# Four reorderings in a fused routing-attention and tanh-shrink kernel: a row of codes ahead of streamed factors, six stores on another queue, one rounding later, routing ahead of one-hot masks

## The chip, the cores and the metric

The kernel runs on one core of a Trainium2 chip. The metric is the device time of one execution in microseconds (us). The core has five engines that run their own instruction streams and wait for each other by semaphores: PE (TensorE, matrix products), DVE (VectorE), ACT (ScalarE), POOL (GpSimd) and SP (SyncE, which here only issues DMAs). Transfers are issued by SP, ACT or POOL, each in its own order, and are carried out by 16 DMA engines.

## The reference

Two blocks follow each other. The first is attention in which a query sees only the keys of its own cluster; the second is a feed-forward layer with the activation h - tanh(h).

```python
# q, k, v: (4, 8, 768, 64); centroids: (8, 16, 64)
q_assign = argmax(q_n @ c_n.T); k_assign = argmax(k_n @ c_n.T)   # per head, 16 clusters
scores = where(q_assign == k_assign, q @ k.T / sqrt(64), -1e9)
attn = softmax(scores)
x = (attn @ v)  -> (3072, 512)          # heads side by side
h = x @ w_in                            # (512, 2048)
out = (h - tanh(h)) @ w_out             # (2048, 512)
```

The weights arrive as 64-bit floats and are rounded to 32 bits on the chip.

## The kernel before, in words

**Steps.** Two heads make a pair; there are 16 pairs, four for each of the four batches. A pair is worked in two halves of 384 queries, and each half in three steps of two blocks of 128 keys. A list `steps` puts them in order: first the halves 0 of pairs 0 to 3 (steps 0 to 11), then their halves 1 (steps 12 to 23), then pair after pair (from step 24). The loop `for at, (n, half, s) in enumerate(steps)` writes out every engine's instructions by hand (`manual_schedule`): the order in the program is the order on each engine and each queue.

In step `at`, PE computes the scores of step `at + 1` (`begin`, line 501), ACT takes their exponentials (line 523), DVE sets those of other clusters to zero (`select`, line 533, which compares a `row` of query codes with a key's code), and PE multiplies the weights of step `at` with the values (`value`, line 558). Between these stand parts of the feed-forward layer (`fill`).

**Masks and codes.** `before(n)` lists the stages of a pair before its first step: turn, `similar` (PE, line 377), `turn_back`, `route` and `route_on` (DVE, lines 387 to 415: the code of each query and key), `publish` (DVE line 432, and a store of the codes by SP, line 436). Pairs 1 to 3 in half 0 have no `select`; PE adds a mask product (line 512) from a one-hot tile `hot`. For that `spread_both` (SP, line 465) reads the codes back into `hot`, and `one_hot` (DVE, lines 476 and 480) turns them into a mask. In step 4 both the one-hot of pair 2 (stage 5) and the routing of pair 3 (stage 2) are due. For the other halves `spread` (SP, lines 448 and 456) fetches a row of codes two to five steps ahead.

**Rounding.** The weights come as 32 pieces. `fetch` asks for one on POOL's queue (line 218), `rest_of` (ACT, lines 150 and 151) and `round_piece` (DVE, lines 159 and 162) round it, and `round_piece` then fetches the piece three further on. `paces` says how many pieces each step rounds.

**Factors.** From batch 0's second half on, the feed-forward products use seven products in place of eight, with sums of quarters of the weights as factors. In steps 20 to 22 `up_maker(0)` and `up_maker(1)` (the index is `q`) make four sums each on DVE (line 833), and `keep` stores these and three plain quarters (numbers 1, 2 and 4, read straight from `w_in`) into `up_factors` in DRAM, each in two DMAs of 256 KB (line 797). The 22 items are dealt out over the three steps, eight, seven and seven. `fetch_factors` (line 856) streams them back into the freed tiles of `w_in`, 896 KB at a time, the first two in step 21 and the next in step 24, where PE begins to use them (`up_product`, line 925; DVE adds in line 920). At the start of step 24 DVE also computes differences of the right side (`right_factors`, line 891) into `w_in[3]`.

Of the kernel before, what the change touches and what calls it, by code (L numbers as in the profile page):

```python
# [58 lines left out]
def kernel(  # L59
# [10 lines left out]
    nc = tc.nc  # L70
# [109 lines left out]
    def fast():  # L180
# [291 lines left out]
        def one_hot(n: int):  # L472


            t = hots[n]
            nc.vector.tensor_scalar(
                out=t[:, 1], in0=t[:, 1], scalar1=mine_code, scalar2=-FAR,
                op0=ALU.not_equal, op1=ALU.mult,
            )
            nc.vector.tensor_scalar(  # L480
                out=t[:, 0, 0], in0=t[:, 0, 0], scalar1=mine_code, scalar2=None, op0=ALU.is_equal
            )
# [42 lines left out]
        def select(n: int, half: int, j: int):  # L525

            if not masked(n, half):
                if j % 2 == 0 and not summed(n, half):
                    weights[n, half, j // 2] = weight_tiles(n, half, j // 2)
                e = weights[n, half, j // 2][j % 2]  # L530
                sc = e if summed(n, half) else scores.pop((n, half, j))
                for h in range(2):
                    nc.vector.scalar_tensor_tensor(  # L533
                        out=e[:, h].rearrange("p (j n) -> p j n", n=P), in0=rows[n, half][:, h],
                        scalar=(
                            codes[n][:, h, 1, j : j + 1] if masked(n, 0) else codes[n][:, 1, j, h : h + 1]
                        ),
                        in1=sc[:, h, 0:TB].rearrange("p (j n) -> p j n", n=P),
                        op0=ALU.is_equal, op1=ALU.mult,
                    )  # L540
            if j % 2 == 1 and not summed(n, half):
                pair = weights[n, half, j // 2]
                if j == 1:
                    s = sums[n, half] = sump.tile([P, 2, TB], F32, name="sum")
                    nc.gpsimd.tensor_tensor(out=s, in0=pair[0], in1=pair[1], op=ALU.add)  # L545
                else:
                    s = sums[n, half]
                    for i in range(2):
                        nc.gpsimd.tensor_tensor(out=s, in0=s, in1=pair[i], op=ALU.add)  # L549
# [232 lines left out]
        HF = CF // 2  # L782
# [7 lines left out]
        def up_maker(q: int):  # L790

            lo, hi = w_in[q], w_in[q + NQ4 // 2]
            a11, a12, a21, a22 = lo[:, 0:CH], lo[:, CH:CD], hi[:, 0:CH], hi[:, CH:CD]

            def keep(which, t):
                for c in range(CH):
                    nc.sync.dma_start(
                        up_factors[
                            q * FQ : (q + 1) * FQ, :, c, SLOT[which]
                        ].rearrange("i p f -> p i f"),  # L800
                        t[:, c].rearrange("p (i f) -> p i f", f=P),
                    )

            return maker(
                (a11, a12, a22), (1, 2, 4),
                ((5, a21, a22, ALU.add), (7, a11, a21, ALU.subtract), (6, 5, a11, ALU.subtract),
                 (3, a12, 6, ALU.subtract)),
                keep, [P, CH, FQ * P],
            )

        def down_maker(q: int):
            lo, hi = w_out[q], w_out[q + NQ4 // 2]
            b11, b12, b21, b22 = lo[:, :, 0:HM], lo[:, :, HM:DM], hi[:, :, 0:HM], hi[:, :, HM:DM]

            def keep(which, t):
                nc.sync.dma_start(
                    down_factors[SLOT[which], :, q * FQ : (q + 1) * FQ], t
                )

            return maker(  # L820
                (b11, b21, b22), (1, 2, 3),
                ((5, b12, b11, ALU.subtract), (7, b22, b12, ALU.subtract), (6, b22, 5, ALU.subtract),
                 (4, b21, 6, ALU.subtract)),
                keep, [P, FQ, HM],
            )

        def maker(quarters, their, sums_, keep, shape):
            made = {}

            def make(which, x, y, op):  # L830
                x, y = (made[i] if isinstance(i, int) else i for i in (x, y))
                t = made[which] = rawp.tile(shape, F32, name="made", tag="raw")
                nc.vector.tensor_tensor(out=t, in0=x, in1=y, op=op)  # L833

            items = []
            for i, args in enumerate(sums_):
                items.append(lambda args=args: make(*args))
                if i < len(quarters):
                    items.append(lambda i=i: keep(their[i], quarters[i]))
                items.append(lambda args=args: keep(args[0], made[args[0]]))  # L840
            return items
# [4 lines left out]
        def fetch_factors(n: int):  # L846

            if n < (B - 1) * PER:
                i = n + HF if n < 0 else n % PER
                t = w_in[(0, 2, 1)[(n + HF) % 3]].rearrange("p c f -> p (c f)")  # L850
                if i < HF:
                    t = t[:, 0 : 7 * CH * P].rearrange("p (c k f) -> p c k f", k=7, c=CH)
                else:
                    t = t[:, 0 : HF * HM].rearrange("p (a b) -> p a b", b=HM)
                streams[n] = t
                nc.sync.dma_start(t, up_factors[i] if i < HF else down_factors[i - HF])
# [225 lines left out]
        HALF = HP * NS  # L1082
# [25 lines left out]
        ready = {}  # L1108
# [109 lines left out]
            load(n, (2,))  # L1218
        select(*steps[0][:2], 1)
        ready[1] = {**ready.get(1, {}), 5: lambda: one_hot(1)}  # L1220


        fills = {HALF: (lambda: plain_items(0), HALF), 2 * HALF: (lambda: plain_items(1), 2 * HALF)}
# [2 lines left out]

        paces = dict(enumerate((0, 1, 1, 1, 1, 1, 2, 1, 2, 1, 1, 0, 3, 2, 2, 2, 2, 2, 2, 3, 2)))
        late, divides, makers, later, listed = [], [], [], {}, []  # L1230
        begun, selected = set(), set()
        fill, whole, spent, since, over = [], 0.0, 0.0, 0, 1
        for at, (n, half, s) in enumerate(steps):
# [6 lines left out]
                whole, spent, since = sum(it[0] for it in fill), 0.0, at  # L1240
            if at == 2 * HALF - 4:
                makers = [it for i in range(2) for it in up_maker(i)]
                half_made = len(makers) // 2
            if at == 2 * HALF:
                makers = [it for i in range(2) for it in down_maker(i)]
            now = []
# [42 lines left out]
            share = paces.get(at, 0)  # L1289
# [46 lines left out]
            todo = []  # L1336
# [36 lines left out]
                light = list(range(at, 2 * HALF - 1))  # L1373
            if makers and at in light:
                share = -(-len(makers) // len(light))
                todo += makers[:share]
                if at < 2 * HALF and len(makers) > half_made >= len(makers) - share:
                    todo += [lambda n=n: fetch_factors(n - HF) for n in range(2)]
                del makers[:share]
            if "raw" in late_pools:  # L1380
                todo += [check_done, check_done, check_on, check_on]
# [9 lines left out]
            if 2 * HALF <= at < 3 * HALF:  # L1391
                masks = 3 if half == 1 and s == NS - 1 else 2
                first_masks, todo = todo[:masks], todo[masks:]
# [212 lines left out]
    with ExitStack() as cx, tc.manual_schedule():  # L1606
        fast()
# [35 lines left out]
```

## Time and profile before

The median of three runs is 954.13 us (953.81 to 956.83). The profiled execution took 951.96 us, and its span, from the first to the last instruction, is 950.2 us.

| | |
|---|---|
| median of three runs | 954.13 us |
| profiled execution | 951.96 us |
| span of the profiled execution | 950.2 us |
| PE busy | 933.2 us, 98% of the span |
| DVE busy | 593.0 us, 62% |
| POOL busy | 511.4 us, 54% |
| ACT busy | 292.9 us, 31% |
| granted TensorE clock, mean | 0.994 |
| DMA | 139.92 MB, 147 GB/s mean |

Engine times are sums over the whole span and hide where an engine stands still. Windows and the timeline show that. SPq in a timeline stands for an instruction that issues a DMA on SP. Its length is the time to issue and not that of the transfer. A clock of 0.50 in a window means that TensorE was granted half its speed.

### The profile page before, as it was taken

The page shows a single profiled execution, that of the slowest core. Times are in us where ns is not written, and L with a number is a line of the kernel's source. Part 1 is how long each engine was busy: PE and PEld are TensorE (multiplying, and loading weights), DVE is VectorE, ACT ScalarE, POOL GpSimd, SP SyncE. Part 2 cuts the span into 40 slices and gives each one's busy share as a digit, 9 for nine tenths or more (in the row PEclk, how much of TensorE's full clock was granted, in tenths as well). Part 3 has the DMA queues.
Part 4 walks back from the last instruction along what each step waited for, and adds up shares of the span by engine and source line. Part 5 has one row for each costly group of instructions (what it writes and reads, how often), then busy time and mean ns, then how long its engine had stood idle before and what let it go on. Part 6 is the DMA issues. An engine that isn't in the chain of part 4 may idle for free.

```text
span 950.2 us, 16920 instructions
## 1 busy us (share of the span) xinstructions
PE 933.2 (98%) x6558; PEld 465.4 (49%) x6558; DVE 593.0 (62%) x1127; ACT 292.9 (31%) x453; POOL 511.4 (54%) x365
## 2 busy tenths in 40 slices
PE   8989999989999999999999999999999999999997
PEld 4434443345553334444466664444456665445664
DVE  6657687877677688657746568766756348443011
ACT  5676554214332222333321112333331220222000
POOL 0126353446585555778686454867797343657500
PEclk9999999989999999999999999999999999999999
DMA  7785464973837645474666646567334222323331
GB/s 177 223 206 138 134 158 128 295 193 101 192 117 183 153 135 124 154 188 110 192 159 203 153 140 206 117 180 182 114 126 149 98 84 100 118 83 128 107 107 37
DMA packets 168456, 139.92 MB, mean 147 GB/s; under 512 B 118272, under 2 KB 146736, under 8 KB 165680
## 3 DMA queue, kind: packets, MB, share of 16 engines
q1 hardware_dynamic: 161984, 117.23, 45.0%
q0 software_dynamic: 6240, 21.50, 7.1%
q8 instruction: 54, 0.88, 0.4%
q14 instruction: 34, 0.28, 0.1%
q10 hardware_dynamic: 144, 0.03, 0.0%
HBM read 117.48 MB, written 21.24 MB: 146 GB/s over the span
## 4 chain that ended last, share of the span: by engine, by line
PE 89%; DVE 5%; DMA 3%; issue 1%; ACT 1%; SPq 1%; POOL 0%; DVEq 0%; POOLq 0%
PE pu L925 27%; PE pd L1030 23%; PE sc L501 13%; PE av L558 13%; PE o L748 5%; PE h L732 4%; PE sim L377 1%; DVE e L533 1%; DMA hot<-q_codes 1%; DMA row<-q_codes 1%; PE den L619 1%; DMA q_codes<-qc 1%; DVE made L833 1%; PE den L592 1%; DVE den L709 1%
## 5 line engine op out<-in xcount | busy, mean ns | idle before, releaser
L549 POOL TENSOR_TENSOR sum<-sum,e 128x768 f32<-128x768 f32 x112 | 206.8, 1846 | 92.5 <-DVE e L533 88.1
L533 DVE SCALAR_TENSOR_TENSOR e<-row,code,sc 128x384 f32<-128x384 bf16 x336 | 185.0, 607 | 79.0 <-ACT sc L523 51.1
L1030 PE MATMUL pd<-w_in,G 128*64 128x256 f32 (+1 forms) x1728 | 191.6, 379 | 0.0
L523 ACT ACTIVATE sc<-sc 128x768 f32<-128x768 f32 x168 | 125.9, 789 | 193.9 <-PE sc L501 165.7
L1030 PEld LDWEIGHTS pd<-w_in,G 128*64 128x64 f32 (+1 forms) x1728 | 130.5, 144 | 61.7 <-issue 5.9
L925 PE MATMUL pu<-xT,w_in 128*64 128x384 f32 (+1 forms) x1024 | 158.9, 447 | 0.6 <-PE pu L925 0.4
L501 PE MATMUL sc<-t,t 64*128 64x384 f32 x768 | 150.6, 510 | 0.2 <-ACT t L363 0.2
L558 PE MATMUL av<-e,vals 128*64 128x384 f32 x768 | 145.0, 499 | 0.0
L994 POOL TENSOR_TENSOR G<-G,th 128x768 f32<-128x768 f32 (+1 forms) x51 | 87.2, 1725 | 67.6 <-ACT th L992 67.5
L925 PEld LDWEIGHTS pu<-xT,w_in 128*64 128x64 f32 x1024 | 73.1, 137 | 74.6 <-issue 61.0
L501 PEld LDWEIGHTS sc<-t,t 64*128 64x128 f32 x768 | 67.2, 187 | 73.7 <-issue 37.5
L925 PE MATMUL pu<-diff,w_in 128*64 128x384 f32 x576 | 101.7, 487 | 0.0
L545 POOL TENSOR_TENSOR sum<-e 128x768 f32<-128x768 f32 x28 | 52.7, 1881 | 78.3 <-DVE e L533 63.0
L558 PEld LDWEIGHTS av<-e,vals 128*64 128x64 f32 x768 | 47.8, 136 | 82.1 <-issue 79.4
L992 ACT ACTIVATE th<-G 128x768 f32<-128x768 f32 (+1 forms) x51 | 40.9, 806 | 148.9 <-DVE G L920 148.6
L748 PE MATMUL o<-w_out,g 128*64 128x512 f32 x384 | 85.8, 592 | 0.0
L925 PEld LDWEIGHTS pu<-diff,w_in 128*64 128x64 f32 x576 | 40.8, 137 | 52.0 <-issue 45.2
L920 DVE TENSOR_TENSOR G<-pu,u 128x384 f32<-128x384 f32 x72 | 39.6, 550 | 27.1 <-PE pu L925 27.1
L748 PEld LDWEIGHTS o<-w_out,g 128*64 128x64 f32 x384 | 27.5, 137 | 50.5 <-issue 50.5
L1047 DVE SCALAR_TENSOR_TENSOR c<-pd,w_in 128x256 f32<-128x256 f32 x36 | 15.1, 419 | 48.9 <-PE pd L1030 48.9
L732 PE MATMUL h<-xT,w_in 128*64 128x384 f32 x256 | 42.8, 486 | 0.0
L1047 DVE SCALAR_TENSOR_TENSOR w_in<-pd,w_in 128x256 f32<-128x256 f32 x31 | 13.0, 419 | 44.8 <-PE pd L1030 44.3
(144 smaller groups left out, 871.3 us busy)
## 6 DMA issues: line engine op xcount, KB each, us to landing
w_in<-up_factors SPq DMA_DIRECT2D x32, 896.0 KB
w_in<-down_factors SPq DMA_DIRECT2D x21, 1024.0 KB
raw<-in_moe_w_in_dram POOLq DMA_DIRECT2D x16, 512.0 KB, 4.9
raw<-in_moe_w_out_dram POOLq DMA_DIRECT2D x16, 512.0 KB, 5.0
again<-in_moe_w_in_dram SPq DMA_DIRECT2D x32, 256.0 KB
again<-in_moe_w_out_dram SPq DMA_DIRECT2D x32, 256.0 KB
vals<-in_v_dram SPq DMA_DIRECT2D x32, 192.0 KB
row<-q_codes SPq DMA_DIRECT2D x29, 192.0 KB
```

What stands on the lines that cost most here:

```text
L501: nc.tensor.matmul(sc[i][:, h, 0:TB], lhsT=turned[n, 1][r].rearrange("p a n -> p (a n)")[:, j * P : (j + 1) * P], rhs=turned[n, 0][r, half ...
L523: nc.scalar.activation(out=out, in_=sc[i][:, :, 0:TB], func=ACT.Exp, scale=SCALE)
L533: nc.vector.scalar_tensor_tensor(out=e[:, h].rearrange("p (j n) -> p j n", n=P), in0=rows[n, half][:, h], scalar=(codes[n][:, h, 1, j : j ...
L545: nc.gpsimd.tensor_tensor(out=s, in0=pair[0], in1=pair[1], op=ALU.add)
L549: nc.gpsimd.tensor_tensor(out=s, in0=s, in1=pair[i], op=ALU.add)
L558: nc.tensor.matmul(avs[n, half][h * D : h * D + D], lhsT=vals[n][:, h, j], rhs=e[i][:, h], start=(j == 0), stop=(j == NCH - 1),)
L732: nc.tensor.matmul(h[r], lhsT=w_in[i][:, c, o * P : (o + 1) * P][:, r], rhs=xT[c][:, half], start=(c == 0), stop=(c == CD - 1),)
L748: nc.tensor.matmul(acc[sub][r], lhsT=gs[f % HF][:, f // HF, sub * P : (sub + 1) * P][:, r], rhs=w_out[f // FQ][:, f % FQ], start=(f == seq ...
L925: nc.tensor.matmul(ps[r], lhsT=streams[base + i][:, c, k_, r], rhs=right[c], start=(c == 0), stop=(c == CH - 1),)
L992: nc.scalar.activation(out=th, in_=t, func=ACT.Tanh)
L994: nc.gpsimd.tensor_tensor(out=t, in0=t, in1=th, op=ALU.subtract)
L1030: nc.tensor.matmul(out_, lhsT=w, rhs=x, start=(i == 0), stop=(i == HF - 1))
```

## The change

There are four edits. In `up_maker(0)`, the stores of the plain quarters 1, 2 and 4, two DMAs each, are issued by ACT in place of SP. In step 4, the routing of pair 3 comes ahead of the one-hot of pair 2 in DVE's order. In `paces`, step 5 rounds no piece instead of one, and step 9 rounds two instead of one. The first two streamed factors are asked for in step 22 ahead of that step's stores, and no more at the end of step 21; step 22 starts with the request for the row of codes of step 24, so on SP the row now comes ahead of the factors.

```diff
@@ up_maker
             def keep(which, t):
+                queue = nc.scalar if q == 0 and which in (1, 2, 4) else nc.sync
                 for c in range(CH):
-                    nc.sync.dma_start(
+                    queue.dma_start(
                         up_factors[
                             q * FQ : (q + 1) * FQ, :, c, SLOT[which]
@@ after the stages are listed
         ready[1] = {**ready.get(1, {}), 5: lambda: one_hot(1)}
+        ready[4][2] = [ready[4][2], ready[4].pop(5)]
@@ ahead of the loop over the steps
-        paces = dict(enumerate((0, 1, 1, 1, 1, 1, 2, 1, 2, 1, 1, 0, 3, 2, 2, 2, 2, 2, 2, 3, 2)))
+        paces = dict(enumerate((0, 1, 1, 1, 1, 0, 2, 1, 2, 2, 1, 0, 3, 2, 2, 2, 2, 2, 2, 3, 2)))
@@ in the loop
                 makers = [it for i in range(2) for it in up_maker(i)]
-                half_made = len(makers) // 2
@@
                 share = -(-len(makers) // len(light))
+                if at == 2 * HALF - 2:
+                    todo += [lambda n=n: fetch_factors(n - HF) for n in range(2)]
                 todo += makers[:share]
-                if at < 2 * HALF and len(makers) > half_made >= len(makers) - share:
-                    todo += [lambda n=n: fetch_factors(n - HF) for n in range(2)]
                 del makers[:share]
```

## The prediction

> **What bounds the kernel now.** I read the page first: PE is busy 933.2 of 950.2 us and the chain that ended last is 89% PE, so time can only be won where PE stands still or runs slowly. Windows of 20 us then place the loss: PE is full except in the first 20 us (start-up), in 40 to 60 us (17.30 of 20), in 200 to 220 us (16.52, at a mean clock of 0.83) and in the tail. The waits of PE alone name the two in the middle:
>
> ```profile
> PE pu L925 <- DVE g L920: 3.5, 1, 3.5
> PE sc L512 <- DMA each<-list: 2.7, 1, 2.7
> ```
>
> The second names the wrong releaser. The timeline around it shows the chain (start, duration, engine, line; in brackets the idle time before):
>
> ```profile
> 37.31 0.69 DVE L162 CUSTOM_DVE_ANT_0 w_in<-w_in,rest 128x1024 uint16<-128x1024 uint16 x1 [4.06 <-ACT rest L151]
> 39.54 0.42 DVE L476 TENSOR_SCALAR hot<-hot,mine_code 128x768 bf16<-128x768 bf16 x1 [1.54 <-DMA hot<-q_codes]
> 40.11 0.59 DVE L387 STREAM_TRANSPOSE sim<-sim 128x384 f32<-128x384 f32 x1
> 44.48 0.14 DVE L432 CAST listed_codes<-code 128x24 bf16<-128x24 f32 x1
> 46.30 0.53 POOL L218 DMA_DIRECT2D raw<-in_moe_w_in_dram  x1 [1.79 <-ACT rest L151]
> 49.02 1.11 SPq L465 DMA_DIRECT2D hot<-q_codes  x2
> 56.52 0.42 DVE L476 TENSOR_SCALAR hot<-hot,mine_code 128x768 bf16<-128x768 bf16 x1 [5.04 <-DMA hot<-q_codes]
> 57.23 0.50 PE L512 MATMUL sc<-hot 64*128 64x384 bf16 x4 [2.69 <-DMA each<-list]
> ```
>
> PE's mask product of step 9 waits for the one-hot of pair 3 (56.52), that for its codes sent out at 49.02, those for the routing of pair 3 at 40.11, and the routing stood behind the one-hot of pair 2, for which VectorE waited 1.54 us. The clock stayed at 1.00: this stall costs 2.69 us and no more.
>
> The first one, in the timeline and two windows (bounds, length, busy time by engine, clock, DMA share, GB/s):
>
> ```profile
> 179.07 1.74 SPq L797 DMA_DIRECT2D up_factors<-made  x2
> 180.98 1.54 SPq L856 DMA_DIRECT2D w_in<-up_factors  x2
> 182.56 0.49 SPq L456 DMA_DIRECT2D row<-q_codes  x1
> 185.70 1.23 DVE L833 TENSOR_TENSOR made<-w_in,made 128x1024 f32<-128x1024 f32 x1 [1.22 <-DMA up_factors<-made]
> 191.10 2.19 DVE L533 SCALAR_TENSOR_TENSOR e<-row,code,sc 128x384 f32<-128x384 bf16 x4 [4.17 <-DMA row<-q_codes]
> 203.31 0.61 DVE L920 TENSOR_TENSOR g<-pu,t 128x192 f32<-128x192 f32 x2
> 203.71 1.55 PE L925 MATMUL pu<-w_in,w_in 128*64 128x192 f32 x8 [3.48 <-DVE g L920]
> ...
> 181.00:191.10 10.10, 10.10 (x54) 3.62 (x51) 4.71 (x4) 2.47 (x4) 3.32 (x3) 1.00 1.02 322
> 203.71:209.13 5.42, 5.42 (x20) 2.48 (x22) 1.79 (x5) 1.59 (x2) 2.41 (x3) 0.50 0.63 101
> ```
>
> The row of codes of step 24 is asked for at 182.56, behind two streamed factors of 896 KB, on a DMA system that is full. VectorE waits 4.17 us for it, then works without a gap from 191.10 to 203.9, and PE has stood since 200.23 for the last of that. PE then runs 5.42 us at half clock: 5.42 x 0.5 = 2.71 us more. This stall costs 3.48 + 2.71 = 6.19 us.
>
> **The Trainium skill.** "TensorE: Matmul & The Clock Gate", Part 1: the clock follows free-running windows of about 3.4 us and halves after an idle one. Here 3.48 us of standing was followed by half clock until 209.13, and 2.69 us by none; it agrees, and it makes the price depend on the phase. "DMA: Bandwidth & Descriptors", "Queues, rings and completion order": SP and ACT each own a ring on each of the same 16 engines, consumed in ring order, the engines going round between rings. So a row behind two factors pays for them; the 8.5 us from issue (182.56) to use (191.10) agrees. The same page, "Issuing engines are not separate DMA queues": a second issuer saves only the issue time. No ACT store is in this trace to show it.
>
> **The change, part by part.**
> *Row ahead of factors.* At step 22 SP's order becomes row, factors, stores, where it was factors, row, stores. From 181.00 to 191.10 the engines moved 10.10 us x 322 GB/s = 3.25 MB; less 2 x 0.9 MB of factors and 0.2 MB of row, some 1.2 MB of stores stood ahead. Then (1.2 + 0.2) / 0.322 = 4.3 us: the row lands at 185.3. A second estimate: the stores issued until 180.81 freed the made tile at about 185.6 (end of the 1.22 us wait); row behind them, 0.2 MB, 186.3. VectorE is free at 185.70 + 1.23 = 186.93, so the row no longer decides: select starts at 186.93 and not 191.10, 4.17 us earlier. The gapless chain then ends at 203.9 - 4.17 = 199.7, before PE's 200.23. Its scores must be there too: the exponentials of step 25 begin at 195.64, and the selects that need them move to 197.04. So the stall goes, with 0.5 us to spare, and with it the cold clock: -6.19. I keep 0.3 us of stall for the thin margin: -5.9. The factors come later by the row, 0.2 MB or 0.6 us: about 186.3 + 1.8 MB / 0.322 = 191.9, PE needs them at 197.46. What stands behind on SP (stores, third factor at 195.08, loads of x) keeps its place.
>
> *Six stores on ACT.* SP loses 1.13 + 1.32 + 1.79 = 4.24 us of issue in step 20. But at 172.36 SP waits for a made tile that VectorE finishes at 176.02, so most of this does not reach the row; bytes are the same. I book 0 for it, up to 1.5 us earlier stores as a margin for the row. ACT gets six issues after 162.88 (end of den), unblocked, as w_in was rounded long before. Price: 0.57 us each as the first pair on SP (1.13 / 2), 0.9 in a full system (1.79 / 2), so 3.4 to 5.4 us. ACT is idle for 2.72 us until 165.60; behind the issues stand the exponentials of step 22, at most 2.7 us late. Their selects on VectorE, 167.67 to 169.85, would end at 172.6 at worst, and PE multiplies those weights at 175.87. Cost 0; uncovered it would be 2.7.
>
> *Routing ahead of one-hot.* VectorE is free at 38.00, sim was ready at 36.89. Routing takes 40.11 to 43.07 = 2.96, so it runs 38.0 to 40.96; one-hot of pair 2 follows until 41.7. PE loads it for step 6 at 41.93: hidden, by 0.2 us; if missed, tenths. VectorE has saved the 1.54 us wait, so the codes of pair 3 go out 1.3 to 1.5 us earlier (44.48 to 43.1).
>
> *Rounding moved from step 5 to step 9.* Steps 6 to 8 keep their counts and each piece slides by one. ACT loses 44.60 to 46.01 and POOL the 512 KB load at 46.30, which ran beside the codes and the one-hot source: those took 56.52 - 50.13 = 6.4 us after issue, where pair 2's took 39.54 - 36.63 = 2.9. So the source is issued at about 47.5 to 48.6 and lands at 51.5 (with 6.4 us: 55.0). The one-hot, behind step 6's rounding on VectorE (ends 51.5), is done at 52.2; PE asks at 54.1. Stall gone: -2.69; with the slow landing 1.2 us remain. At step 9 the piece adds 1.56 us on ACT and 1.1 us on VectorE. ACT: exponentials of step 11 0.4 us late, PE needs their bank 1.5 us later: hidden. VectorE runs gapless from 61.83 to 72.8, where selects of step 12 free the score banks; PE came for them at 72.47, with 0.77 us of slack for the first and 0.45 for the second. 1.1 us more costs 1.1 - 0.45 = 0.65. Its load on POOL falls near 61, where the DMA share drops to 0.25 and then to nothing until 63.
>
> Sum: -5.9 - 2.69 + 0.65 = -7.9 us, against the profiled execution of 951.96 (span 950.2, 1.76 around it): 944.0. The median of the timed runs, 954.13, lies 2.17 above it, and they spread by 3 us, about one cold stretch; I take the difference over: 946.2.
>
> **Rivals.** (a) *The row is late all the same*, since 1.2 MB of stores stand ahead anyway: landing 189 instead of 186.3 leaves 1.4 us of stall, without cold clock; the gain is 6.19 - 1.4 + 2.04 = 6.8, 947.3. The same if the subtractions into w_in[3] wait for stores that read it. For it: DMA share 1.02. Against: the made tile's release at 185.6. (b) *Only one stall goes.* If the one-hot source stays slow: 2.69 - 1.2 - 0.65 = 0.8 and 5.9, 947.4. If only the first goes: 954.13 - 2.04 = 952.1. (c) *No effect*: a new wait of equal size where a stall was, 954. (d) *Slower: ACT's issue.* SP's longest single store took 2.69 us. Six such, 16.1 us from 162.88, end at 179.0; exponentials 180.5, selects 182.7, and PE, due at 175.87, stands 6.8 us and goes cold for 3.4 more: 10.2 lost. VectorE's whole chain is late, so the old stall may partly remain, 2 us: 951.96 - 2.04 - 6.19 + 10.2 + 2 = 955.9, median 958. It starts to cost above (2.72 + 6.02) / 6 = 1.46 us an issue and decides near 2.5. Against: at 163 the DMA system had just been at a share of 0.40.
>
> **How the numbers follow.** Likeliest, both stalls go: 0.58, 946.2, own range 943 to 949. (a) and slow source 0.18, near 947.4. Only the first stall 0.06, 952.1; no effect 0.08; slower 0.10, from 957 up. 0.3% of 954.13 is 2.86 us, about what a measurement of this kernel can tell from no change: faster is below 951.27. Faster 0.58 + 0.18 + 0.04 = 0.80, same 0.10, slower 0.10. The low end takes both stalls whole and the spread of timed runs: 954.13 - 8.9 - 2.2 = 943. The high end, 952.5, leaves out slower and no effect.
>
> **What would show it.** Right: in PE's waits neither 3.5 nor 2.7 us; VectorE's wait for the row gone, and the clock at 1.00 around 200 us; one-hot of pair 3 done before PE asks; six stores on ACT under 1 us each. Wrong: PE waiting for exponentials at step 22, a wait on hot or row of the old length, a new stall near step 13 over 1 us, or an early gain that a later wait gives back.

## The result and the profile after

The changed kernel takes 948.88 us (median of seven runs, 946.9 to 952.04), the kernel before in the same session 955.2 us (median of seven, 953.81 to 956.99). The ratio is 0.9937, with a 95% interval of 0.9919 to 0.9955: 0.6% faster, where 0.8% was forecast; between the medians lie 6.3 us. The profiled execution took 946.9 us with a span of 944.8 (before: 951.96 and 950.2). PE is busy for 931.7 us, and its mean clock is 0.998.

In the changed kernel every line named here from 796 on is one higher: `up_product` 926, its additions 921, the sums of factors 834, the stores of factors 798. The waits of PE in the changed kernel (engine, operation and line, the releaser; then us in total, times, longest):

```profile
PE pu L926 <- DVE g L921: 1.9, 1, 1.9
...
PE sc L501 <- ACT e L523: 0.8, 1, 0.8
...
PE sc L501 <- DVE e L533: 0.5, 1, 0.5
```

The 2.7 us before the mask product are gone. The 3.5 us in step 25 have shrunk to 1.9, not to nothing, and two short waits for scores are new. The timeline of the changed kernel shows each. First the one-hot of pair 3 (start, duration, engine, line, operation; in brackets the idle time before and its releaser):

```profile
37.75 0.59 DVE L387 STREAM_TRANSPOSE sim<-sim 128x384 f32<-128x384 f32 x1
40.63 0.41 DVE L476 TENSOR_SCALAR hot<-hot,mine_code 128x768 bf16<-128x768 bf16 x1
42.66 0.14 DVE L432 CAST listed_codes<-code 128x24 bf16<-128x24 f32 x1
46.30 1.11 SPq L465 DMA_DIRECT2D hot<-q_codes  x2
51.24 0.41 DVE L476 TENSOR_SCALAR hot<-hot,mine_code 128x768 bf16<-128x768 bf16 x1
54.20 0.49 PE L512 MATMUL sc<-hot 64*128 64x384 bf16 x4
```

The routing starts at 37.75 where it started at 40.11, the source of the one-hot is asked for at 46.30 where it was 49.02, and the mask product at 54.20 waits for nothing.

Then steps 9 to 12, with the rounding that was moved into step 9:

```profile
59.06 0.57 POOL L218 DMA_DIRECT2D raw<-in_moe_w_in_dram  x1 [0.41 <-ACT rest L151]
60.67 5.78 SPq L341 DMA_DIRECT2D x<-in_q_dram  x4
64.46 0.80 ACT L150 ACTIVATE rest<-raw 128x512 uint16<-128x512 uint32 x1 [1.80 <-DMA raw<-in_moe_w_in_dram]
65.75 1.48 ACT L523 ACTIVATE e<-sc 128x768 f32<-128x768 f32 x2
66.58 1.62 PE L501 MATMUL sc<-t,t 64*128 64x384 f32 x8 [0.80 <-ACT e L523]
70.90 1.96 PE L501 MATMUL sc<-t,t 64*128 64x384 f32 x8 [0.48 <-DVE e L533]
```

ACT stands 1.80 us for the weights of the piece (64.46), which POOL asked for only at 59.06. The exponentials of step 11 stand behind it (65.75), and PE waits 0.80 us for the score bank that they free.

Last, steps 20 to 25. ACTq is an instruction that issues a DMA on ACT:

```profile
163.63 4.60 ACTq L798 DMA_DIRECT2D up_factors<-w_in  x3
164.34 3.45 SPq L798 DMA_DIRECT2D up_factors<-made  x4
168.35 1.50 ACT L523 ACTIVATE sc<-sc 128x768 f32<-128x768 f32 x2 [6.71 <-DMA up_factors<-made]
169.25 2.19 DVE L533 SCALAR_TENSOR_TENSOR e<-row,code,sc 128x384 f32<-128x384 bf16 x4 [2.67 <-ACT sc L523]
182.45 0.86 SPq L456 DMA_DIRECT2D row<-q_codes  x1
183.42 2.12 SPq L857 DMA_DIRECT2D w_in<-up_factors  x2
188.33 2.19 DVE L533 SCALAR_TENSOR_TENSOR e<-row,code,sc 128x384 f32<-128x384 bf16 x4 [0.26 <-DMA row<-q_codes]
200.54 0.62 DVE L921 TENSOR_TENSOR g<-pu,t 128x192 f32<-128x192 f32 x2
200.95 0.87 PE L926 MATMUL pu<-w_in,w_in 128*64 128x192 f32 x8 [1.88 <-DVE g L921]
```

The row now comes ahead of the factors (182.45 before 183.42) and DVE waits 0.26 us for it instead of 4.17. But the exponentials of step 22 begin at 168.35, and DVE stands 2.67 us for them; it works from 188.33 to 200.54 all but without a gap (12.11 of 12.21 us busy), and PE waits 1.88 us for its end. What PE is spared is the half clock afterwards, in the windows of the changed kernel (bounds, length, busy time of PE, PEld, DVE, ACT and POOL, clock, DMA share, GB/s):

```profile
200.95:206.37 5.42, 5.42 (x52) 2.88 (x54) 3.02 (x7) 1.50 (x2) 3.82 (x3) 1.00 1.07 262
```

To see where the time went I cut PE's timeline at marks that all kernels share: stretch I from the start to the mask product of step 8, II up to the scores computed in step 19 (the expectations below call them the scores of step 19; they are those for step 20), then 51.2 to 51.3 us that hardly differ, III from the scores of step 25 to those of step 27, and the rest. All in us, from one profiled execution each; the last columns are the timed runs, each against the kernel before on the same chip.

| kernel | I | II | III | rest | span | timed median | ratio [95% interval] |
|---|---|---|---|---|---|---|---|
| before | 50.33 | 93.08 | 19.02 | 736.56 | 950.2 | 955.2 | |
| changed | 50.16 | 92.09 | 14.78 | 736.55 | 944.8 | 948.88 | 0.9937 [0.9919, 0.9955] |
| e1: six stores back on SP | 51.70 | 92.07 | 13.24 | 735.97 | 944.2 | 946.39 | 0.9895 [0.9835, 0.9955] |
| e2: row first, alone | 50.16 | 94.01 | 12.68 | 735.93 | 944.0 | 950.44 | 0.9937 [0.9909, 0.9964] |
| e3: stores on ACT, alone | 50.23 | 98.33 | 20.09 | 736.33 | 956.2 | 957.81 | 1.0008 [0.9990, 1.0027] |
| e9: four stores on ACT | 50.15 | 92.41 | 13.16 | 736.46 | 943.4 | 945.58 | 0.9891 [0.9866, 0.9916] |
| e5: rounding moved, alone | 50.61 | 94.68 | 18.43 | 735.86 | 950.8 | 953.66 | 0.9983 [0.9961, 1.0006] |
| e10: routing first and row first | 50.39 | 90.21 | 13.09 | 735.99 | 940.9 | 943.25 | 0.9866 [0.9843, 0.9890] |
| e4: rounding at step 11 | 53.04 | 91.73 | 15.80 | 736.41 | 948.2 | 947.42 | 0.9895 [0.9835, 0.9955] |
| e8: stores on SP, rounding at step 13 | 50.16 | 90.55 | 12.68 | 735.89 | 940.5 | 942.45 | 0.9863 [0.9843, 0.9883] |
| a1: changed, once more | 50.29 | 93.41 | 17.38 | 736.53 | 948.9 | 951.03 (one run) | |
| a2: changed, once more | 51.65 | 92.85 | 17.41 | 736.07 | 949.2 | 951.33 (one run) | |

Of the 5.4 us that the span lost, stretch III gave 4.24, II 0.99 and I 0.17. The theory to be tested was that row first and routing first bring the gain, and that the stores on ACT and the moved rounding each give some of it back.

### The profile page after: what moved, and what is told of

Same layout as the page of the kernel before. It is cut to its first block, busy times and chain, and to the rows that moved or that the text cites. A ratio compares the mean times of both kernels' runs of the same rounds, so it can differ in the third digit from the quotient of the medians.

```text
span 944.8 us, 16918 instructions
## 1 busy us (share of the span) xinstructions
PE 931.7 (99%) x6558; PEld 464.9 (49%) x6558; DVE 593.3 (63%) x1127; ACT 292.9 (31%) x453; POOL 512.4 (54%) x365
## 4 chain that ended last, share of the span: by engine, by line
PE 88%; DVE 5%; DMA 3%; ACT 1%; issue 1%; SPq 1%; ACTq 0%; DVEq 0%; POOL 0%; POOLq 0%
PE pu L926 27%; PE pd L1031 22%; PE sc L501 13%; PE av L558 12%; PE o L748 5%; PE h L732 4%; DVE e L533 1%; PE sim L377 1%; PE den L619 1%; DVE den L709 1%; PE warm L303 1%; DMA up_factors<-made 1%; DMA row<-q_codes 1%; DVE made L834 1%; DMA raw<-in_moe_w_in_dram 1%
## 5 line engine op out<-in xcount | busy, mean ns | idle before, releaser
L558 PEld LDWEIGHTS av<-e,vals 128*64 128x64 f32 x768 | 47.5, 136 | 81.1 <-issue 79.1
```

What stands on the lines that cost most here:

```text
L558: nc.tensor.matmul(avs[n, half][h * D : h * D + D], lhsT=vals[n][:, h, j], rhs=e[i][:, h], start=(j == 0), stop=(j == NCH - 1),)
```

## The experiments

### Step 22 is late: is it the stores on ACT? (e1)

The changed kernel with all stores on SP:

```diff
-                queue = nc.scalar if q == 0 and which in (1, 2, 4) else nc.sync
+                queue = nc.sync
```

> The changed kernel with all stores of factors back on SP; the other three edits stay. Theory 1 (ACT): the 1.88 us of PE's stall that are left near 200 us come from the six stores on ACT; the exponentials of step 22 stood behind them (168.35 where 164.4 was due), VectorE waited 2.67 us for them and its gapless chain up to 200 us was late by that. Then here ACT's exponentials of step 22 start at about 164.4, VectorE uses the row near 185.8 (188.33 in the changed kernel), PE's stall is 0 to 0.3 us, the span 944.8 - 1.7 = 943. Theory 2 (backlog): the row lands at about 188 because the stores stand ahead of it whoever issues them, and SP has 4.2 us more to issue; then the row is used at 188 or later, the stall is 1.9 us or more and the span 944.8 or more.

The timeline of e1:

```profile
164.19 0.69 DVE L162 CUSTOM_DVE_ANT_0 w_out<-w_out,rest 128x1024 uint16<-128x1024 uint16 x1 [1.08 <-ACT rest L151]
...
165.96 1.50 ACT L523 ACTIVATE sc<-sc 128x768 f32<-128x768 f32 x2 [1.10 <-issue]
...
188.32 2.19 DVE L533 SCALAR_TENSOR_TENSOR e<-row,code,sc 128x384 f32<-128x384 bf16 x4 [0.44 <-DMA row<-q_codes]
...
200.93 0.87 PE L926 MATMUL pu<-w_in,w_in 128*64 128x192 f32 x8 [0.34 <-DVE g L921]
```

The exponentials of step 22 are on time, PE's stall falls from 1.88 to 0.34 us and III from 14.78 to 13.24. So the stores on ACT cost 1.54 us in these two executions. (The timed ratios of the two kernels, 0.9895 and 0.9937, have intervals that overlap and don't tell them apart.) The row's use did not move to where I had written it: stretch I is 1.5 us longer here, and against the scores of step 25 the use comes 6.67 us ahead where it came 5.14 ahead in the changed kernel. It could come about 1 us earlier still (7.74 in e2 below): here DVE waits 1.08 us for the rounding of a piece of the second weight, ahead of the sums (the line at 164.19), which it does neither in e2 nor in the changed kernel.

Why ACT was held up that long does not follow from the length of an issue: one took 0.37 to 0.57 us here. The list of waits of the built program names the reason. DMAHW0 to DMAHW7 are eight completion semaphores that the DMAs of SP and ACT take in turn; a DMA that takes one up again waits until the earlier transfer on it has landed. In ACT's order (trimmed; the last line but one is SP's):

```
ACT 154 L798 DMACopy up_factors<-w_in  [waits DMAHW0]
ACT 155 L798 DMACopy up_factors<-w_in  [waits DMAHW2]
ACT 156 L798 DMACopy up_factors<-w_in  [waits DMAHW3]
SP   87 L798 DMACopy up_factors<-made  [waits DMAHW3, DVE]
ACT 157 L523 Activation sc<-sc
```

DMAHW3, on which the sixth store waits, belongs to SP's first store of a made tile, and that one waits for the first sum on DVE. In the changed kernel the sum took from 162.30 to 164.32, SP issued its store at 164.34, and ACT could issue the sixth store only at 167.87; then came the exponentials. The trace agrees: SP and ACT use eight completion semaphores in it, the sixth store waits for the one that SP's store of 164.34 raises, and the last rise came at 167.84. (In e3, e4, a1 and a2, which have the six stores on ACT too, 0.02 to 0.03 us lie between these two events.) The Trainium skill, "DMA: Bandwidth & Descriptors", section "Anatomy of one DMA — SWDGE (gpsimd) path", says that a wait on a semaphore happens on the sequencer that issues, before dispatch, and not in the DMA engines. The section is about DMAs issued by GpSimd; here the trace shows the same of ACT, which stood for 6.71 us before it came to the exponentials.

### Are the last two stores enough to cause it? (e9)

If that wait is the cause, four stores on ACT, which wait for DMAHW 2, 4, 6 and 0, should cost nothing:

```diff
-                queue = nc.scalar if q == 0 and which in (1, 2, 4) else nc.sync
+                queue = nc.scalar if q == 0 and which in (1, 2) else nc.sync
```

> The changed kernel with four stores on ACT (quarters 1 and 2) and those of quarter 4 back on SP. The built program gives the DMAs of SP and ACT eight completion semaphores in turn, and a DMA waits until the last one on its semaphore has landed; the sixth store on ACT waited so for a store that SP issues only after VectorE's first sum. Theory: without it the exponentials of step 22 start when their scores are ready, VectorE does not wait 2.67 us for them, and PE's time from the scores of step 25 to those of step 27 falls from 14.8 us to 12.7 to 13.3. Rival: it is the number of issues on ACT, or the DMA system being full, and four of six leave two thirds: 14 us or more.

The timeline of e9:

```profile
164.75 1.50 ACT L523 ACTIVATE sc<-sc 128x768 f32<-128x768 f32 x2 [1.27 <-PE sc L501]
...
199.63 0.87 PE L926 MATMUL pu<-w_in,w_in 128*64 128x192 f32 x8 [0.25 <-DVE g L921]
```

The exponentials wait for nothing but the scores of PE, the stall is 0.25 us, III is 13.16, as with no store on ACT in e1 (13.24). Four issues are hidden. Of the two that are not, the sixth is the one that waited: in the changed kernel the fifth was out by 164.57. The timed runs agree: 0.9891, with an interval that lies below that of the changed kernel (0.9919 to 0.9955).

### The stores on ACT alone (e3)

The kernel before with that one line (the opposite of the diff of e1):

> The kernel before with one edit: the six stores of plain quarters on ACT. Theory 1: a loss. The exponentials of step 22 are late by about 4 us, VectorE's chain by 2.7 us, the row is still behind the factors; PE's stall near 200 us grows from 3.48 to 5 to 6 us with the cold clock as before, span 951.5 to 953. Theory 2 (SP's issue was the limit, and ACT relieves it): the row comes 1 to 2 us earlier, the stall shrinks to 1.5 to 2.5 us, span 945 to 948.

The timeline of e3:

```profile
59.81 0.82 PE L512 MATMUL sc<-hot 64*128 64x384 bf16 x4 [5.37 <-DVE hot L480]
...
175.43 2.19 DVE L533 SCALAR_TENSOR_TENSOR e<-row,code,sc 128x384 f32<-128x384 bf16 x4 [2.60 <-ACT sc L523]
...
198.35 2.19 DVE L533 SCALAR_TENSOR_TENSOR e<-row,code,sc 128x384 f32<-128x384 bf16 x4 [4.17 <-DMA row<-q_codes]
...
205.39 1.85 PE L926 MATMUL pu<-xT,w_in 128*64 128x192 f32 x20 [1.38 <-DVE xT L712]
...
210.96 1.10 PE L926 MATMUL pu<-w_in,w_in 128*64 128x192 f32 x8 [3.73 <-DVE g L921]
```

DVE waits 2.60 us for the late exponentials here too, and III is 1.07 us longer than before. The other 5.25 us of stretch II are not the edit's: they are the old stall for the one-hot, 5.37 us this time with a cold clock behind it, in code that equals that of before. ACT's delay does not disappear in the wait for the row: DVE waits 4.17 us for it, as before, because SP asks for the row 2.6 us later as well (against the scores of step 25), and it is used 1.43 us ahead of the scores of step 25 (3.53 before). PE stands 1.38 + 3.73 = 5.11 us where it stood 3.48. That III grows by 1.07 and not by these 1.63 is because less of it was at half clock (a mean clock of 0.92 in III, before 0.82). The timed ratio, 1.0008, shows no loss that can be measured; the timed runs of both kernels spread by 9 to 11 us.

### Row first, alone (e2)

The kernel before with the factors asked for in step 22, ahead of its stores:

```diff
+                if at == 2 * HALF - 2:
+                    todo += [lambda n=n: fetch_factors(n - HF) for n in range(2)]
                 todo += makers[:share]
-                if at < 2 * HALF and len(makers) > half_made >= len(makers) - share:
-                    todo += [lambda n=n: fetch_factors(n - HF) for n in range(2)]
```

> The kernel before with one edit: the first two streamed factors asked for behind the row of codes. Theory 1 (the row behind the factors was the whole of the late stall, and ACT is now untouched): the row is used at about 186.9, PE's stall near 200 us is 0 to 0.5 us instead of 3.48, the clock there stays at 1.00, the stall of 2.69 us at 54 us stays; span 950.2 - 6 = 944.2. Theory 2 (backlog of stores): the row is used only 1.5 to 2 us earlier, a stall of 1.5 to 2.5 us is left, span 945.5 to 947.

The timeline of e2:

```profile
57.77 0.50 PE L512 MATMUL sc<-hot 64*128 64x384 bf16 x4 [3.41 <-DVE hot L480]
...
187.65 2.19 DVE L533 SCALAR_TENSOR_TENSOR e<-row,code,sc 128x384 f32<-128x384 bf16 x4 [0.40 <-DMA row<-q_codes]
...
201.57 1.56 PE L501 MATMUL sc<-t,t 64*128 64x384 f32 x8
```

The late stall is gone altogether: III falls from 19.02 to 12.68, 6.34 us. The row is used 7.74 us ahead of the scores of step 25 (195.39 in this execution); in the frame of before, where these begin at 194.62, that is 186.88. The early stall is still there, as it should be: 3.41 us. The profiled execution, 945.79 us, is the second fastest of twelve (943.16 to 955.42); the medians, 950.44 and 956.05, lie 5.6 us apart.

### The early stall: routing or the load that step 5 no longer has? (e5, e10)

I had two changes for one stall, the routing ahead of the one-hot and a load of 512 KB fewer beside the codes. e5 is the kernel before with the new paces alone:

```diff
-        paces = dict(enumerate((0, 1, 1, 1, 1, 1, 2, 1, 2, 1, 1, 0, ...
+        paces = dict(enumerate((0, 1, 1, 1, 1, 0, 2, 1, 2, 2, 1, 0, ...
```

> The kernel before with one edit: the rounding of step 5 at step 9. Theory: the load of 512 KB no longer runs beside the codes and the one-hot source, so the source lands about 3 us after its issue instead of 6.4, and the stall falls from 2.7 (to 5.4 in another execution) to under 1 us; the second piece at step 9 costs its 1.3 to 1.6 us, so from the mask product of step 8 to the scores of step 19 92 to 93 us. The late stretch is that of the kernel before, 19 us. Rival: what shortens the wait is the earlier routing; then the stall stays at 2.7 us or more and the stretch takes 94 us or more.

The timeline of e5:

```profile
56.51 0.42 DVE L476 TENSOR_SCALAR hot<-hot,mine_code 128x768 bf16<-128x768 bf16 x1 [4.74 <-DMA hot<-q_codes]
...
57.21 0.50 PE L512 MATMUL sc<-hot 64*128 64x384 bf16 x4 [2.39 <-DVE hot L480]
...
73.94 1.61 PE L501 MATMUL sc<-t,t 64*128 64x384 f32 x5 [1.42 <-DVE e L533]
```

The one-hot is as late as before (56.51, before 56.52), the stall 2.39 us, and a stall of 1.42 us has joined it at the scores of step 13. II is 1.60 us longer than before. Taking this load away was not enough to make the codes earlier: their source, asked for at 49.31, landed 7.1 us later (before 7.4), beside the loads of step 6, asked for at 50.10 and 51.41.

e10 is the kernel before with the row first, as in e2, and the routing first; the rounding stays in step 5:

```diff
+        ready[4][2] = [ready[4][2], ready[4].pop(5)]
```

> The kernel before with two edits: routing ahead of the one-hot masks, and the factors behind the row of codes; the roundings and the stores as before. Theory: routing first sends the codes 1.4 us earlier, but the 512 KB load of step 5's rounding still runs beside them, so the stall on the one-hot of pair 3 shrinks by about 1.5 us from the 2.7 to 5.4 us seen, and no stall comes at steps 12 and 13: from the mask product of step 8 to the scores of step 19 91.5 to 93 us; the late stretch 12.7 to 13.3 us. Rival: the routing is most of that gain and the load is none: the stall is gone, and this stretch takes 90.5 us.

The timeline of e10:

```profile
46.68 1.11 SPq L465 DMA_DIRECT2D hot<-q_codes  x2
...
52.80 0.42 DVE L476 TENSOR_SCALAR hot<-hot,mine_code 128x768 bf16<-128x768 bf16 x1 [1.24 <-DMA hot<-q_codes]
...
54.43 0.49 PE L512 MATMUL sc<-hot 64*128 64x384 bf16 x4
```

DVE still waits 1.24 us for the source, which takes 6.1 us from issue to one-hot (before 7.5), but it was asked for 2.3 us earlier, and PE does not wait. The load seems to count for the landing too: with the routing first and no load in step 5 (the changed kernel, e1, e4, e8, e9, a1 and a2) the source landed 3.8 to 4.1 us after its issue, with the routing first and that load 6.0 (this one execution), with the old order 7.1 to 7.4. PE does not need that gain. II is 90.21, 2.87 us less than before and 1.88 less than in the changed kernel. Two of the four edits thus make the kernel 1.3% faster than before, twice the gain of all four; the intervals of the two ratios do not overlap.

### Where the rounding can stand (e4, e8)

e4 is the changed kernel with the piece in step 11 instead of step 9:

```diff
-        paces = dict(enumerate((0, 1, 1, 1, 1, 0, 2, 1, 2, 2, 1, 0, 3, 2, ...
+        paces = dict(enumerate((0, 1, 1, 1, 1, 0, 2, 1, 2, 1, 1, 1, 3, 2, ...
```

> The changed kernel with the moved rounding at step 11 instead of step 9. Theory: the stalls of 0.80 us (scores of step 12 behind late exponentials, which stood behind a rounding that waited 1.80 us for its weights) and 0.48 us (scores of step 13 behind VectorE) come from the second piece at step 9; here both go or shrink to under 0.3 us in sum, and the span is 944.8 - 1.2 = 943.6. Rival: ACT and VectorE have as much to do before step 13 as ever, so the same 1.3 us of stall appears at steps 12 to 14, and the span stays at 944.8.

The timeline of e4:

```profile
74.32 2.07 DVE L162 CUSTOM_DVE_ANT_0 w_in<-w_in,rest 128x1024 uint16<-128x1024 uint16 x1 [1.34 <-ACT rest L151]
...
79.53 0.87 PE L732 MATMUL h<-xT,w_in 128*64 128x384 f32 x4 [1.49 <-DVE xT L712]
```

The two waits for scores are gone and another has come: DVE waits 1.34 us for the piece, the division that makes `xT` (line 712) stands behind it, and PE waits 1.49 us for it. II is 91.73, hardly better than 92.09. The rival, that the wait only moves, was right. In this execution the one-hot of pair 2 was late as well (PE 1.21 us, in stretch I), which its one edit, in later steps, does not explain. The late stall is 2.89 us, and the clock stays at full speed behind it.

e8 puts the piece into step 13 and all stores on SP:

```diff
-                queue = nc.scalar if q == 0 and which in (1, 2, 4) else nc.sync
+                queue = nc.sync
-        paces = dict(enumerate((0, 1, 1, 1, 1, 0, 2, 1, 2, 2, 1, 0, 3, 2, ...
+        paces = dict(enumerate((0, 1, 1, 1, 1, 0, 2, 1, 2, 1, 1, 0, 3, 3, ...
```

> The changed kernel with all stores on SP and the moved rounding at step 13 instead of step 9 (step 13 rounds three pieces; its weights are first used later). From the mask product of step 8 to the scores of step 19 on PE the changed kernel takes 92.1 us; with no stall it would be about 90.5. Theory: the 1.6 us more are the second piece of step 9 between the one-hot stage and step 13, where ACT and VectorE have no slack; at step 13 PE has long feed-forward products to hide it, so this stretch takes 90.5 to 90.9 us, the late stretch stays near 13.2 us, and the span is near 942.5. Rival: the piece is late wherever it is put and stalls a first product or an exponential again; the stretch stays near 92 us, the span near 944.

The timeline of e8, the scores that waited in the changed kernel and those of step 26 after the late stall:

```profile
65.72 1.56 PE L501 MATMUL sc<-t,t 64*128 64x384 f32 x8
...
69.43 1.56 PE L501 MATMUL sc<-t,t 64*128 64x384 f32 x8
...
198.11 1.56 PE L501 MATMUL sc<-t,t 64*128 64x384 f32 x8
```

None of them waits. II is 90.55 and III 12.68. At 942.45 us it is the fastest by a hair: 1.4% faster than before and, by the two ratios, some 0.7% faster than the changed kernel; e10, at 943.25, is within its interval. The runs of both lie close together (942.2 to 944.3), those of the kernel before on the same chip far apart (952.9 to 960.4).

### The changed kernel once more (a1, a2)

Its seven timed runs spread over 5 us. Two further executions of the same code should show where:

> The changed kernel once more, unaltered: its profiled execution was the shortest of its seven (946.9, median 948.88). Theory: what differs between executions of it is waiting on transfers, at the places already named; the stretch from the mask product of step 8 to the scores of step 19 takes 92 to 94 us (the roundings near step 9 waiting for their weights), the late stretch 14.5 to 18 us (a larger stall near 200 us may turn the clock cold), and the last 736 us do not differ by more than 0.6 us. Rival: the difference is spread over the whole span, and the last stretch differs by 2 us or more.

> The changed kernel a third time, unaltered; the same is expected as of the run before it: differences of up to 5 us, all of them ahead of 215 us.

The timeline of a1, and its window after the late stall (columns as above):

```profile
72.35 1.97 PE L501 MATMUL sc<-t,t 64*128 64x384 f32 x8 [2.44 <-DVE e L533]
...
203.47 0.87 PE L926 MATMUL pu<-w_in,w_in 128*64 128x192 f32 x8 [2.88 <-DVE g L921]
204.27 2.93 PE L501 MATMUL sc<-t,t 64*128 64x384 f32 x8
```

```profile
203.47:210.00 6.53, 6.53 (x48) 3.22 (x48) 3.21 (x7) 1.59 (x2) 4.19 (x3) 0.74 1.17 260
```

Both spans are 4.1 to 4.4 us longer than that of the profiled execution, and all of it lies in the first 215 us. In a1 it lies at the places of the two costs; in a2, 1.49 us of it lie in stretch I, ahead of all four edits, as in e1. The wait for the scores of step 13 is 2.44 us (a2: 1.95) instead of 0.48. The late stall is 2.88 us (a2: 2.89) instead of 1.88, and PE then runs cold: 6.53 x (1 - 0.74) = 1.7 us more. The first profile of the changed kernel was a lucky one, the fastest of its seven timed runs: stretches II and III both took longer in these two. What of III's 2.6 us more is due to the stores on ACT was not tested; in both, DVE also waited 0.95 to 1.08 us for the same late rounding as in e1, here ahead of the wait for the exponentials (2.48 and 2.15 us).

## Why the prediction was right or wrong

The direction and the place of the gain were right, 2.7 us of its size was not: 948.88 against 946.2, within the range of 943 to 952.5. The distance of the median from the profiled execution was taken over as 2.17 and is 1.98, so the miss lies in the sum: -7.9 forecast, and 951.96 - 946.9 = -5.06 measured. That a single profile shows 5.06 is partly luck: against a1 and a2 it would be less than 1 us, though the medians of one session lie 6.3 apart.

| step of the prediction | forecast | measured |
|---|---|---|
| row ahead of factors | -5.9 (-6.19 in full) | -6.34 alone (e2, III) |
| six stores on ACT | 0 | +1.54 (changed against e1, III), +2.10 (against e2); a1 and a2 against e1: 4.1 to 4.2, half clock included |
| routing first, rounding out of step 5 | -2.69 | -2.87 (e10 against before, II) |
| rounding into step 9 | +0.65 | +1.88 (changed against e10), +1.60 (e5 against before), 2.6 to 3.2 (a2 and a1 against e10), all II |

- **Row ahead of factors: right, mechanism and size.** The select on the row was to start at 186.93; it did at 186.88 in the frame of before. Rival (a), a row that is late all the same, fell: of 4.17 us a wait of 0.26 to 0.44 is left in the changed kernel, e1 and e2.
- **"Cost 0" for the stores on ACT: the step that failed.** I took the six issues for unblocked and the exponentials for at most 2.7 us late; against the scores of step 25 they were 3.9 us later than in e1. And I set them against PE's need of the weights at 175.87, and there the slack was real. But the selects that follow them stand at the head of DVE's work for the sums, the row and the additions, and it was the end of this chain, 25 us later, that PE waited for. A delay of 2.7 us on DVE went through it nearly whole: against the scores of step 25 the row was used 2.6 us later than in e2 (5.14 and 7.74 us ahead). The chain's margin of 0.5 us, which I had worked out for the row one paragraph earlier, was the number to compare with. The price of an issue was wrong in the other direction: 0.37 to 0.57 us, up to 0.73 in e4, e9, a1 and a2, and not 0.57 to 0.9. That ACT would be held by a landing was not among the bounds; rival (d) named the place, but by the length of issues, and these stayed short.
- **Routing ahead of one-hot: right, with too much credit to the load.** No stall, as forecast, and the source was asked for a little earlier (46.30) than my 47.5 to 48.6. I had counted on a fast landing from the load that step 5 lost, and it came: 3.9 us in place of 7.4. But it was not needed. e5 shows that taking the load away does not end the stall by itself (2.39 us), and e10 that the routing does, with a landing of 6.0 us.
- **Rounding at step 9: the term was mis-sized, 0.65 for 1.6 to 3.2.** I took DVE's slack for the price and called ACT's 0.4 us hidden. ACT was later than that since it waited 1.80 us for the piece, whose load landed 5.4 us after its issue beside loads of `x`; I had judged that the DMA system would be quiet there. The exponentials of step 11 stand behind that wait, and so PE waited at two scores, 0.80 and 0.48 us.

In the changed kernel as it stands the terms add to -6.34 + 1.54 - 2.87 + 1.88 = -5.8; its span lost 5.4. With the stores measured against e2 (2.10) they add to -5.23, and with the -0.17 of stretch I to -5.4. e1 is the poorer base, since its III is 0.56 us above that of e2: its chain on DVE began with the wait of 1.08 us for a rounding, more than the chain's margin. That wait is 1.04 us in e10 and 0.95 in e9, whose III are 13.09 and 13.16, and 0.57 in e8, whose III is 12.68. Why that piece comes late in some executions stays open.

The clock, that I tied to the length of the stall with reserve, behaved so: cold behind 3.48, 3.72, 3.73 and 5.37 us, and behind 2.88 and 2.89 in a1 and a2; at full speed behind 2.69, 3.41 (e2) and another 2.89 (e4). The Trainium skill, "TensorE: Matmul & The Clock Gate", Part 1, says that the windows by which the clock is set, of about 3.4 us, run freely. The runs agree in so far as the length of a stall alone does not decide: 2.89 us was followed by both. That the phase decides was not measured. In the prediction a stall that is left of the late one (rival (a), 1.4 us) came without a half clock; one of 2.9 us cost its own length or, in a1, 1.7 us more.

## What to carry to other kernels

Price a late instruction at the end of the longest gapless chain behind it, not at its first reader: here the reader had slack of several us, and the chain had 0.5. A DMA moved to a compute engine costs that engine not only the issue but every landing that the issue must wait for, so read what its semaphore was last used for; the first four stores were free, and the next two cost 1.5 us or more. Where two edits aim at one stall, try each alone: one of the two was enough, and the other, at the place it was given, made its stretch 1.6 us longer or more.

## What was unexpected of the hardware

- An issue on ACT is short (0.37 to 0.57 us in the changed kernel), but six of them took from 160.12 to 168.24, for the waits between them. The Trainium skill, "DMA: Bandwidth & Descriptors", section "Issuing engines are not separate DMA queues", promises from a second issuer only the time of issuing; here SP was spared the six issues, and stretch III grew by 1.5 us against e1 (2.1 against e2).
- A stall of 2.9 us was followed by a half clock twice and by the full clock once.
- The same code met quite different landings of small transfers: the stall for the one-hot of pair 3 was 2.69, 3.41 and 5.37 us in three executions that have the roundings and the order of before. No profiled execution with the routing first shows it. That this is why the runs of e8 and e10 lie closer together is argued and not shown.
